# Four batches interleaved in a traced order, with q cast on DVE, full-row tails and k times v per head in column halves

## The chip, the cores and the metric

The kernel runs on one core of one Trainium2 chip. The metric is the device time of one execution in microseconds; lower is better. Engines are named as in the profile: PE is the tensor engine (PEld its weight loads), DVE the vector engine, ACT the scalar engine, POOL the GpSimd engine, SP the engine that issues most transfers. Rounds of different kernels were taken on the same chip in turn.

## The reference

```python
kv  = einsum('bhsd,bhse->bhde', k, v)            # B=8, H=8, S=576, D=64
out = einsum('bhsd,bhde->bhse', q, kv)
x   = out / sqrt(mean(out*out, -1) + 1e-6) * g_norm   # then heads side by side: [B, S, 512]
theta = x @ w_theta
y = w_tok_r @ (x * cos(theta)) + w_tok_i @ (x * sin(theta))   # over tokens
u = x + y
return u + maximum(u @ w_ch, 0)
```

The eight batches are independent. 576 rows are four blocks of 128 and a tail of 64.

## The kernel before

Each batch runs four stages: attention (k·v, transposes of q, q·kv, the norm), phase (transposes of x, theta, sin and cos), mix (token product), channel (last product). The driver interleaves two batches, and the scheduler may reorder within that.

```python
def attention(b):
    kvp = ps([P, HP, P], FP32, f"kv{b}")
    for hp in range(HP):                          # a pair of heads
        pair = slice(2 * hp, 2 * hp + 2)
        ks = work.tile([P, NF, 2, D], FP32, tag="ks", bufs=4, ...)
        nc.gpsimd.tensor_copy(ks[:].rearrange("p j h d -> p h j d"), kt[:, pair, :, :])   # L171
        qs = work.tile([P, NT, 2, D], FP16, tag="qs", bufs=4, ...)
        nc.gpsimd.tensor_copy(qs[:, 0:NF].rearrange(...), qt[:, pair, :, :])
        nc.gpsimd.tensor_copy(qs[:T, NF], ql[:, pair, :])                  # T = 64 rows
        for j in range(NT):
            lhs = ks[:, j, :, :] if j < NF else kl[:, pair, :]
            rhs = vt[:, pair, j, :] if j < NF else vl[:, pair, :]
            nc.tensor.matmul(kvp[:, hp, :], lhs, rhs, ...)                 # L180, half of the result unused
        # transposes of q: four full blocks and two 64x64 ones for the tail (L185)
        ...
    # the two diagonal blocks of kvp go to bd (ACT, L194)
    for ti in range(NT):
        raw = ...                                 # PE, L202: q times bd
        nc.scalar.activation(out=sq, in_=raw, func=AFT.Square)
        nc.vector.reduce_sum(out=ss, in_=sq, ...)
        nc.gpsimd.tensor_scalar(out=ss, in0=ss, scalar1=D * eps, op0=ALU.add)
        nc.gpsimd.tensor_tensor(out=rt, in0=ss, in1=mhalf, op=ALU.pow)
        nc.vector.tensor_tensor(out=xt, in0=raw, in1=rt, op=ALU.mult)      # L219
...
attention(0); load(1, 1); phase(0); token_weights()
for b in range(B):
    if b + 1 < B:
        attention(b + 1)
        if b + 2 < B: load(b + 2, 1)
    if b > 0: channel(b - 1)
    mix(b)
    if b + 1 < B: phase(b + 1)
channel(B - 1)
```

## Time and profile before

381.67 us median of three runs (377.65 to 382.21).

| | busy in one round of 41.64 us | share |
|---|---|---|
| PE | 34.18 us | 82% |
| DVE | 23.97 us | 58% |
| ACT | 19.56 us | 47% |
| POOL | 16.62 us | 40% |

The first fence is from the page of the kernel before: busy microseconds with the share of the span, then 40 equal slices with the busy share in tenths, and the clock granted to PE.

```profile
PE 291.6 (76%) x1965; PEld 176.1 (46%) x1965; DVE 186.2 (49%) x348; ACT 164.4 (43%) x283; POOL 133.5 (35%) x191
...
PE   0097267993996699669968699569968899759895
...
PEclk9999997568798699788997899688997899899999
```

Next, busy time by stretch for one round, taken between equal points of two batches. The columns are the stretch, its length, the busy time of each engine with the number of instructions, the granted clock, the DMA share and GB/s.

```profile
core 0: us, PE busy (x) PEld busy (x) DVE busy (x) ACT busy (x) POOL busy (x), PEclk, DMA share, GB/s
...
187.02:228.66 41.64, 34.18 (x241) 20.39 (x240) 23.97 (x42) 19.56 (x34) 16.62 (x22) 0.88 0.40 115
```

The waits of PE in this round (who waited for whom; us in total, times, longest):

```profile
PE raw_0_1833 L202 <- ACT kvbd_106 L194: 3.8, 1, 3.8
PE vps_4_1982 L330 <- DVE x_3_1887 L219: 1.7, 1, 1.7
PE ups_4_1975 L322 <- DVE x_2_1873 L219: 1.3, 1, 1.3
PE vps_2_1952 L330 <- DVE x_1_1859 L219: 0.7, 1, 0.7
```

And the chain of waits that ended last, by engine:

```profile
PE 43%; DVE 20%; POOL 16%; ACT 10%; DMA 6%; issue 4%; POOLq 0%; DVEq 0%; ACTq 0%
```

No engine is full, and the chain wanders over all of them. PE stands 3.8 us for the eviction of kv and 3.7 us for x in every round. The gaps also cost clock. Right after the 3.8 us wait the q·kv matmuls start 107 ns apart, and at full clock such 128-column matmuls start 56 ns apart. The Trainium skill (TensorE: Matmul & The Clock Gate, Part 1) says that the array falls to half clock after an idle window of about 3.4 us. In this trace less was enough: PE's last matmul before the wait ends at 196.9 us, and the granted clock falls to 0.50 at 199.0 us, 2.1 us later. The mean granted clock of the round is 0.88.

The packed copies and q casts on POOL stretch DVE operations: of these equal instructions (groups by line, shapes kept apart; busy us, mean ns) the first ran beside a q cast on POOL and the second beside nothing.

```profile
L265 DVE TENSOR_SCALAR fa_3_1730<-f_3_1728 128x512 int32<-128x512 int32 x1 | 0.8, 827 | 0.0
...
L265 DVE TENSOR_SCALAR fa_0_1673<-f_0_1671 128x512 int32<-128x512 int32 x1 | 0.4, 421 | 0.0
```

And a k·v group looks like this: eight records of 128 columns for the four blocks of one pair.

```profile
L180 PE MATMUL kv_1754<-v_1459,ks_2_1793 128*128 128x128 f32 x8 | 1.2, 288 | 0.0
```

### The profile page before, as it was taken

To read this page: it belongs to the slowest core of one execution; us is meant where nothing else is said; L and a number is where in the kernel's file an instruction comes from. 1 tells how busy PE (TensorE), PEld (TensorE's weight loads), DVE (VectorE), ACT (ScalarE), POOL (GpSimd) and SP (SyncE) were. 2 spreads that over 40 slices of the span, in tenths; PEclk is the share of its full clock that TensorE was granted. 3 is DMA by queue.
4 is the path that set the end of the run, shared out by engine and by line. 5 is a ranking of instruction groups with operands and counts; after the bars stand their busy time and mean duration, and the time that the engine had idled before them with its cause. 6 is when DMAs were issued, how large, how long until landed. Compare 5 with 4: busy or idle time off the path is not lost.

```text
span 381.3 us, 5161 instructions
## 1 busy us (share of the span) xinstructions
PE 291.6 (76%) x1965; PEld 176.1 (46%) x1965; DVE 186.2 (49%) x348; ACT 164.4 (43%) x283; POOL 133.5 (35%) x191
## 2 busy tenths in 40 slices
PE   0097267993996699669968699569968899759895
PEld 0076125761574256534555357424644357425352
DVE  0001418025494456546484639346564638463954
ACT  1026049340486118711674139610864149513902
POOL 2254640366074503461065406460156300540000
PEclk9999997568798699788997899688997899899999
DMA  8999980069009230753029220502000210021033
GB/s 155 231 323 300 284 236 0 2 160 320 20 8 309 87 95 2 193 167 129 11 87 270 82 58 2 138 27 99 3 0 0 91 35 2 0 80 47 0 125 124
DMA packets 44760, 40.98 MB, mean 107 GB/s; under 512 B 14144, under 2 KB 39360, under 8 KB 44736
## 3 DMA queue, kind: packets, MB, share of 16 engines
q1 hardware_dynamic: 43760, 38.80, 35.8%
q0 software_dynamic: 976, 1.85, 2.7%
q8 instruction: 15, 0.25, 0.3%
q14 instruction: 9, 0.07, 0.1%
HBM read 33.06 MB, written 9.44 MB: 111 GB/s over the span
## 4 chain that ended last, share of the span: by engine, by line
PE 43%; DVE 20%; POOL 16%; ACT 10%; DMA 6%; issue 4%; POOLq 0%; DVEq 0%; ACTq 0%
PE kv_138 L180 3%; PE kv_494 L180 3%; DMA wnat_124<-in_moe_w_tok_i_dram 2%; DMA wnat_123<-in_moe_w_tok_r_dram 2%; PE kv_3089 L180 2%; PE y_0_1102 L303 1%; DMA out_dram<-ot_1_3549 1%; PE y_0_2437 L303 1%; ACT tr_l L284 1%; PE y_0_1547 L303 1%; PE y_0_2882 L303 1%; ACT kvbd_108 L194 1%; ACT kvbd_106 L194 1%; PE y_0_1992 L303 1%; DMA out_dram<-ot_1_3265 1%
## 5 line engine op out<-in xcount | busy, mean ns | idle before, releaser
L180 PE MATMUL kv_138<-v_68,ks_0_139 128*128 128x128 f32 x8 | 2.1, 441 | 19.5 <-POOL ks_0_139 L171 19.5
L109 DVE TENSOR_SCALAR gcol<-gcol 128x1 f32<-128x1 f32 x1 | 0.2, 153 | 25.2 <-DMA gcol<-in_g_norm_dram 25.2
L180 PEld LDWEIGHTS kv_138<-v_68,ks_0_139 128*128 128x128 f32 x8 | 1.8, 328 | 19.5 <-POOL ks_0_139 L171 19.5
L190 ACT COPY qT_0_156<-qTps_0_149 128x640 f16<-128x640 f16 x1 | 0.7, 692 | 21.1 <-PE qTps_0_149 L185 21.1
L214 POOL TENSOR_SCALAR ss_0_3175<-ss_0_3175 128x8 f32<-128x8 f32 x1 | 0.2, 238 | 26.5 <-DVE ss_0_3175 L209 26.5
L242 ACT ACTIVATE xT_741<-xTps_0_742,gcol 128x640 f16<-128x640 f16 x1 | 0.8, 794 | 15.9 <-PE xTps_0_742 L237 15.9
L209 DVE TENSOR_REDUCE ss_0_580<-sq_0_578 128x8 f32<-128x512 f32 x1 | 0.7, 686 | 13.6 <-ACT sq_0_578 L207 13.6
L171 POOL COPY ks_0_1755<-k_1458 128x512 f32<-128x512 f32 x1 | 0.6, 609 | 17.4 <-PE kv_1309 L180 17.4
L171 POOL COPY ks_0_3090<-k_2793 128x512 f32<-128x512 f32 x1 | 0.6, 609 | 17.4 <-PE kv_2644 L180 17.4
L171 POOL COPY ks_0_2200<-k_1903 128x512 f32<-128x512 f32 x1 | 0.6, 609 | 16.3 <-PE kv_1754 L180 16.3
L171 POOL COPY ks_0_2645<-k_2348 128x512 f32<-128x512 f32 x1 | 0.6, 609 | 16.1 <-PE kv_2199 L180 16.1
L242 ACT ACTIVATE xT_299<-xTps_0_300,gcol 128x640 f16<-128x640 f16 x1 | 0.8, 794 | 11.9 <-PE xTps_0_300 L237 11.9
L171 POOL COPY ks_0_865<-k_643 128x512 f32<-128x512 f32 x1 | 0.6, 610 | 14.9 <-PE kv_494 L180 14.9
L306 PE MATMUL yl_656<-wT_428,z_0_345 128*128 128x64 f16 x4 | 0.9, 230 | 6.4 <-DVE uT_655 L310 6.4
L303 PEld LDWEIGHTS <-z_l 128*128 128x128 f16 x32 | 3.3, 103 | 3.9 <-issue 0.8
L171 POOL COPY ks_0_1310<-k_1013 128x512 f32<-128x512 f32 x1 | 0.9, 904 | 11.8 <-PE kv_864 L180 11.8
L209 DVE TENSOR_REDUCE ss_0_224<-sq_0_222 128x8 f32<-128x512 f32 x1 | 0.7, 686 | 8.6 <-ACT sq_0_222 L207 8.6
L327 ACT COPY u_0_3688<-ups_0_3683 128x512 f16<-128x512 f16 x1 | 0.6, 586 | 9.7 <-PE ups_0_3683 L322 9.7
L330 PEld LDWEIGHTS <-uT_655 128*128 128x128 f16 (+1 forms) x20 | 2.2, 119 | 5.4 <-issue 3.8
L242 ACT ACTIVATE xT_1186<-xTps_0_1187,gcol 128x640 f16<-128x640 f16 x1 | 0.8, 793 | 8.6 <-PE xTps_0_1187 L237 8.6
L250 PEld LDWEIGHTS <-xT_299 128*128 128x128 f16 x20 | 2.4, 126 | 4.5 <-issue 2.9
L242 ACT ACTIVATE xT_2521<-xTps_0_2522,gcol 128x640 f16<-128x640 f16 x1 | 0.8, 793 | 8.6 <-PE xTps_0_2522 L237 8.6
(1960 smaller groups left out, 1187.3 us busy)
## 6 DMA issues: line engine op xcount, KB each, us to landing
k_67<-in_k_dram SPq DMA_DIRECT2D x4, 256.0 KB, 9.3
v_68<-in_v_dram SPq DMA_DIRECT2D x4, 256.0 KB, 10.5
q_69<-in_q_dram SPq DMA_DIRECT2D x4, 256.0 KB, 10.1
k_287<-in_k_dram SPq DMA_DIRECT2D x1, 1024.0 KB, 7.1
v_288<-in_v_dram SPq DMA_DIRECT2D x1, 1024.0 KB, 8.3
q_289<-in_q_dram SPq DMA_DIRECT2D x1, 1024.0 KB, 11.2
k_643<-in_k_dram SPq DMA_DIRECT2D x1, 1024.0 KB, 10.2
v_644<-in_v_dram SPq DMA_DIRECT2D x1, 1024.0 KB, 9.9
```

The source lines that it names most:

```text
L171: nc.gpsimd.tensor_copy(ks[:].rearrange("p j h d -> p h j d"), kt[:, pair, :, :])
L180: nc.tensor.matmul(kvp[:, hp, :], lhs, rhs, start=(j == 0), stop=(j == NT - 1))
L190: nc.scalar.copy(out=t[:], in_=pq[:])
L194: nc.scalar.copy(out=bd[r * D:(r + 1) * D, :, r * D:(r + 1) * D], in_=kvp[r * D:(r + 1) * D, :, r * D:(r + 1) * D],)
L209: nc.vector.reduce_sum(out=ss[:], in_=sq[:].rearrange("p (h e) -> p h e", h=H), axis=mybir.AxisListType.X,)
L242: nc.scalar.activation(out=xT[:, kc, :], in_=px[:], func=AFT.Copy, scale=gcol[:])
L250: nc.tensor.matmul(th[:], xT[:, kc, ti * P:(ti + 1) * P], wth[:, kc, :], start=(kc == 0), stop=(kc == NK - 1),)
L284: nc.scalar.activation(out=tr[:], in_=f[:], func=AFT.Sin, scale=-RAD, bias=tail_bias[:])
L303: nc.tensor.matmul(y[:], lhs, wT[n][:, 0:SF], start=(n == 0), stop=(n == 2 * NF))
L306: nc.tensor.matmul(yl[:, kc, :], lhs, wT[n][:, SF:S], start=(n == 0), stop=(n == 2 * NF))
L327: nc.scalar.copy(out=u[:rows], in_=pu[:rows])
L330: nc.tensor.matmul(vp[:rows], uT[:, kc, ti * P:ti * P + rows], wch[:, kc, :], start=(kc == 0), stop=(kc == NK - 1),)
```

## The change

The intent: let stages of four batches interleave in one order that is traced by a virtual clock (each stage of batch b has a window in rounds of 28 us), and hold every engine to that order; and take work off PE and POOL. k·v is now computed per head, each head's 64 columns in one half of the array, which needs no packed copy of k and computes no unused half; q is cast on DVE; tails are padded to full rows so that no 64-row matmul is left in k·v and in the transposes. The core of the diff, with cuts:

```diff
+ROUND = 28.0
+WINDOWS = {"cast": (-1.0, 13.0), "attention": (0.0, 14.0), "norm": (17.0, 44.0), "turn": (45.0, 53.0),
+    "phase": (52.0, 78.0), "mix": (82.0, 110.0), "channel": (112.0, 140.0)}
+def in_traced_order(tc):                 # each instruction after the last one traced on its engine
+    ...
-    psA = ctx.enter_context(tc.tile_pool(name="psA", bufs=8, ...))
+    PS = {"kv": 1, "raw": 2, "tp": 2, "mm": 3}          # PSUM banks
-            nc.gpsimd.tensor_copy(ks[:].rearrange("p j h d -> p h j d"), kt[:, pair, :, :])
-            nc.gpsimd.tensor_copy(qs[:, 0:NF]..., qt[:, pair, :, :])
+        nc.vector.tensor_copy(st["qs", b][:, 0:NF, 2 * hp:2 * hp + 2, :]..., qs[hp][:])
-                nc.tensor.matmul(kvp[:, hp, :], lhs, rhs, ...)
+            for r in range(2):
+                nc.tensor.matmul(
+                    kvp[r * D:(r + 1) * D, hp, :],
+                    ks[hp][:, r, j, :] if j < NF else kl[:, 2 * hp + r, :],
+                    vs[hp][:, r, j, :] if j < NF else vl[:, 2 * hp + r, :],
+                    start=(j == 0), stop=(j == NT - 1),
+                )
-            for (j, rows, at) in blocks:                # 4 full blocks, 2 of 64 rows
+        for j in range(NT):                             # 5 full blocks
                 nc.tensor.matmul(pq[...], ..., is_transpose=True, ...)
...
+    load(0)
+    load_theta()
+    for b in range(B):
+        if b > 0:
+            put((b - 0.9) * ROUND, once(load, b))
+        for (name, (stage, n)) in stages.items():
+            (lo, hi) = WINDOWS.get((name, b), WINDOWS[name])
+            for i in range(n):
+                put(b * ROUND + lo + (hi - lo) * i / n, stage(b, i))
+    put(0.9 * ROUND, once(load_mixers))
+    ...                                                 # stages run in order of virtual time
+    in_traced_order(tc)
```

Also the token mix is split in halves of 288 columns in place of 512 and 64, q, k and v are loaded per pair of heads (a q tail twice), the token weights are loaded later, and the eight PSUM banks are given to fixed uses (1, 2, 2 and 3).

## The prediction

> **What bounds it now.** No engine: the order does. The chain of waits repeats: 41.9, 41.6, 42.9 and 42.4 us between equal points of batches 3 to 7. From 187.0 to 228.7 us (busy time by stretch) PE is busy 34.2 us, DVE 24.0, ACT 19.6, POOL 16.6. The chain that ended last is PE 43%, DVE 20%, POOL 16%, ACT 10%: one batch's norm (square, reduce, pow of 1.67 us, scale) and phase run while PE has little other work. The PE timeline shows 3.8 us waiting for the kv eviction and 3.7 us for x per batch, and gaps cost clock: mean granted 0.88, raw matmuls 107 ns apart instead of 56. The first k·v matmul starts at 19.5 us, behind 16.8 us of token-weight loads on the chain.
>
> **What changes.** Four batches interleave, so PE finds work during those waits. Per batch, from full-clock spacings in the PE timeline:
> - k·v: 40 records 150 ns apart, tails slower (0.21 us): 6.3 us now. Afterwards 80 records with half the columns. The Trainium skill (TensorEngine Tiling (Array Packing), Key Properties) says different tiles run in parallel but a mode switch drains the array; no run shows it yet. Estimate 4.5 us (3 if the halves overlap, 6.5 if not).
> - q and x transposes: 2 x 1.96 us to 2 x 1.1, as half-row tails go.
> - token mix: 36 x 0.216 + 36 x 0.028 = 8.8 us to 72 x 0.122 = 8.8 us (estimate).
> - raw 1.1, theta 4.3, channel 5.4: unchanged.
>
> PE sum about 27 us (29.5 now, without waits and cold clock).
> - DVE: the q cast comes, 5 x 128x512 f32, estimated at the 0.42 us of the 128x512 bit-and: 2.1 us. POOL's copies (7.4 us) go, and with them the DVE operations stretched beside them (0.74 to 1.06 us instead of 0.42). DVE about 25 us; POOL keeps 9.5, ACT 20.
> - Token weights load later; a q tail is loaded twice.
>
> **On the critical path.** Nearly all of it: the round becomes the larger of PE 27 and DVE 25 us, plus stalls of in-order queues: 29.5 us instead of 42. By the traced windows a batch spans five rounds: four filling, four full, four draining. Filling is bound by loads: 3.7 MB per batch plus weights at the 250 to 300 GB/s of the first 60 us gives 75 to 85 us until the fifth batch starts. Full: 4 x 29.5 = 118 us. Draining: PE sums of 20, 18, 13 and 5 us plus latency, about 70 us. End transfer 4 us.
>
> **Predicted: 275 us, range 255 to 305 (8 in 10). Faster by over 2%: 0.97; within: 0.02; slower: 0.01.**
>
> **What would show each step.** PE busy over 85% with a granted clock above 0.95 in the middle; rounds of 28 to 31 us; first k·v matmul before 10 us; k·v group 3 to 6.5 us per batch; cast at 0.42 us (0.7 at half rate, DVE then 26.5); no bit-and above 0.5 us; PE's waits for x and kvbd gone.
>
> **What would make it wrong.** A fixed order stalls one engine on another (PE on a bank that ACT or DVE still reads: two transposing, three product banks), rounds then being 33 us or more; column halves that do not overlap and drain the array at each switch; loads and stores sharing one queue, a waiting load delaying stores; filling slower than loads allow, from latency and a cold clock.

## More of the kernel before

The kernel before shows runs near 376 us and near 382 us, the latter with a lower mean granted clock (0.89 and 0.93 are typical), and the later ones of that kind were counted as slow.

The profiled run spans 381.3 us: it took 383.09 us at a mean granted clock of 0.886, so it is like the runs that were later counted as slow. The rounds and waits of the kernel before are read from it and may be up to some 2% too long (the fast runs are near 376 to 378 us).

## The result

286.76 us median of four runs (286.23 to 288.16); before, 379.66 us (376.42 to 382.21). The ratio is 0.758, with a 95% interval from 0.750 to 0.766. Ratios here are the mean time of one kernel's fast runs over that of the other's of the same rounds, so not quite the ratio of the medians. The profiled run spans 284.7 us.

The lines of the page after that answer to those before (busy, slices, clock, chain by engine):

```profile
PE 226.5 (80%) x2221; PEld 154.7 (54%) x2221; DVE 191.8 (67%) x396; ACT 168.6 (59%) x283; POOL 81.0 (28%) x91
...
PE   1053463866489888998999899989999988999994
...
PEclk9997575599859999999999999999999999999999
...
PE 36%; DVE 25%; ACT 16%; POOL 10%; issue 5%; DMA 5%; SPq 2%; ACTq 0%; DVEq 0%
```

Busy time by stretch, cut at the kv eviction of each batch (found to 0.5 us; the DMA share adds up the time that packets took, and can pass 1), so that each line but the last is one round; two middle rounds, equal to the one shown, are left out:

```profile
core 0: us, PE busy (x) PEld busy (x) DVE busy (x) ACT busy (x) POOL busy (x), PEclk, DMA share, GB/s
0.00:24.50 24.50, 7.05 (x100) 5.85 (x101) 4.51 (x17) 5.97 (x9) 0.69 (x6) 1.00 0.90 234
24.50:45.00 20.50, 9.96 (x124) 8.11 (x123) 7.02 (x14) 5.85 (x12) 10.97 (x13) 0.60 1.06 251
45.00:72.00 27.00, 17.54 (x198) 12.39 (x199) 15.85 (x36) 18.28 (x31) 9.80 (x10) 0.80 1.09 278
72.00:98.00 26.00, 20.01 (x199) 13.38 (x198) 18.38 (x39) 17.50 (x30) 9.64 (x10) 0.80 0.46 115
98.00:123.50 25.50, 23.26 (x255) 16.11 (x253) 21.68 (x46) 18.88 (x33) 9.61 (x10) 1.00 0.38 98
123.50:151.00 27.50, 26.06 (x274) 17.80 (x273) 23.01 (x49) 20.03 (x35) 9.60 (x10) 1.00 0.63 173
...
206.00:284.70 78.70, 70.53 (x534) 45.50 (x532) 55.29 (x107) 41.98 (x71) 11.46 (x12) 1.00 0.20 69
```

The longest wait of PE in the middle, from 123 to 206 us, which are three rounds and have three such waits:

```profile
PE ups_4_2139 L366 <- ACT xT_2078 L296: 0.8, 1, 0.8
...
```

And the groups that changed: the sixteen k·v records of one pair (two heads), one bit-and, one cast.

```profile
L230 PE MATMUL kv_1768<-v_2_1376,k_2_1375 128*64 128x64 f32 x16 | 0.7, 228 | 0.0
...
L325 DVE TENSOR_SCALAR fa_2_1957<-f_2_1955 128x512 int32<-128x512 int32 x1 | 0.4, 426 | 0.0
...
L216 DVE CAST qs_1745<-q_1_1371 128x512 f16<-128x512 f32 x1 | 0.4, 418 | 0.0
```

The middle is a different machine: rounds of 27.5 us with PE busy 26.07 (95%), clock 1.00, no waits for x or kv left, and 1.4 us of idle PE a round. The first five rounds are not: PE is busy 7.05 + 9.96 + 17.54 + 20.01 + 23.26 = 77.8 of their 123.5 us. Of the 58 us in which PE idles in the whole span, 45.7 lie there, 4.3 in the middle and 8.2 at the end.

### The profile page after: what moved, and what is told of

Its sections match the earlier page's. It is cut to its first block, busy times and chain, and to the rows that moved or that the text cites. A ratio compares the mean times of both kernels' runs of the same rounds, so it can differ in the third digit from the quotient of the medians.

```text
span 284.7 us, 5734 instructions
## 1 busy us (share of the span) xinstructions
PE 226.5 (80%) x2221; PEld 154.7 (54%) x2221; DVE 191.8 (67%) x396; ACT 168.6 (59%) x283; POOL 81.0 (28%) x91
## 4 chain that ended last, share of the span: by engine, by line
PE 36%; DVE 25%; ACT 16%; POOL 10%; issue 5%; DMA 5%; SPq 2%; ACTq 0%; DVEq 0%
DMA k_2_118<-in_k_dram 2%; DMA wst_133<-in_moe_w_theta_dram 2%; SPq L135 1%; DMA wst_142<-in_moe_w_theta_dram 1%; SPq L143 1%; ACT xT_3328 L296 1%; ACT xT_2541 L296 1%; ACT xT_2078 L296 1%; ACT xT_2975 L296 1%; ACT xT_1615 L296 1%; PE y_0_878 L351 1%; ACT xT_806 L296 1%; ACT xT_1172 L296 1%; DVE uT_3415 L356 1%; ACT wth L170 1%
## 5 line engine op out<-in xcount | busy, mean ns | idle before, releaser
L170 ACT ACTIVATE wth<-wst_133 128x512 f16<-128x512 f32 x1 | 0.6, 630 | 15.0 <-DMA wst_133<-in_moe_w_theta_dram 15.0
L238 PE MATMUL qTps_0_159<-ident_75,qs_145 128*128 128x128 f16 x5 | 0.7, 309 | 9.0 <-DVE qs_145 L216 9.0
L238 PEld LDWEIGHTS <-qs_145 128*128 128x128 f16 x20 | 1.5, 116 | 10.4 <-DVE qs_145 L216 9.2
L267 DVE TENSOR_REDUCE ss_0_262<-sq_0_260 128x8 f32<-128x512 f32 x1 | 0.7, 686 | 8.1 <-ACT sq_0_260 L264 8.1
L238 PEld LDWEIGHTS <-qs_288 128*128 128x128 f16 x20 | 1.6, 125 | 6.1 <-DVE qs_288 L216 6.0
L230 PE MATMUL kv_148<-v_0_103,k_0_102 128*64 128x64 f32 x16 | 1.1, 319 | 4.4 <-DMA v_0_103<-in_v_dram 4.4
L304 PEld LDWEIGHTS <-xT_1172 128*128 128x128 f16 x20 | 1.9, 98 | 4.0 <-ACT xT_1172 L296 2.3
L304 PEld LDWEIGHTS <-xT_806 128*128 128x128 f16 x20 | 1.9, 106 | 3.4 <-ACT xT_806 L296 2.4
L230 PE MATMUL kv_148<-vl_68,kl_67 128*64 128x64 f32 x16 | 1.6, 296 | 2.7 <-DMA vl_68<-in_v_dram 2.7
L238 PEld LDWEIGHTS <-qs_528 128*128 128x128 f16 x20 | 1.1, 98 | 4.4 <-DVE qs_528 L216 4.2
L304 PEld LDWEIGHTS <-xT_2975 128*128 128x128 f16 x20 | 1.9, 98 | 2.7 <-ACT xT_2975 L296 0.7
L304 PEld LDWEIGHTS <-xT_3328 128*128 128x128 f16 x20 | 1.9, 98 | 2.7 <-ACT xT_3328 L296 0.7
L230 PEld LDWEIGHTS kv_148<-v_0_103,k_0_102 128*64 128x64 f32 x16 | 1.0, 221 | 4.4 <-DMA k_0_102<-in_k_dram 4.4
L258 PE MATMUL raw_2_291<-kvbd_89,qT_0_165 128*128 128x128 f16 x1 | 0.3, 288 | 3.8 <-DVE x_0_267 L278 3.8
L291 PE MATMUL xTps_0_441<-ident_75,x_4_438 128*128 128x128 f16 x1 | 0.3, 287 | 3.8 <-DVE x_4_438 L278 3.8
L304 PEld LDWEIGHTS <-xT_2078 128*128 128x128 f16 x20 | 1.9, 98 | 2.5 <-ACT xT_2078 L296 0.7
L304 PEld LDWEIGHTS <-xT_2541 128*128 128x128 f16 x20 | 1.9, 98 | 2.5 <-ACT xT_2541 L296 0.7
L304 PEld LDWEIGHTS <-xT_1615 128*128 128x128 f16 x20 | 1.9, 98 | 2.5 <-ACT xT_1615 L296 0.7
L304 PEld LDWEIGHTS <-xT_440 128*128 128x128 f16 x20 | 1.9, 105 | 2.3 <-ACT xT_440 L296 0.7
L304 PE MATMUL th_0_870<-wth,xT_806 128*128 128x512 f16 x4 | 2.3, 619 | 1.0 <-ACT xT_806 L296 1.0
## 6 DMA issues: line engine op xcount, KB each, us to landing
wnat_97<-in_moe_w_tok_i_dram POOLq DMA_DIRECT2D x1, 576.0 KB, 11.7
```

What stands on the lines that cost most here:

```text
L170: nc.scalar.activation(out=wth[:, kc, :], in_=wst[:], func=AFT.Copy, scale=FOLD)
L230: nc.tensor.matmul(kvp[r * D:(r + 1) * D, hp, :], ks[hp][:, r, j, :] if j < NF else kl[:, 2 * hp + r, :], vs[hp][:, r, j, :] if j < NF els ...
L238: nc.tensor.matmul(pq[:, j * P:(j + 1) * P], st["qs", b][:, j, pair, :], ident16[:], is_transpose=True, start=(j == 0), stop=(j == NT - 1),)
L258: nc.tensor.matmul(raw[:, hp * P:(hp + 1) * P], st["qT", b, hp][:, ti * P:(ti + 1) * P], bd[:, hp, :], start=(hp == 0), stop=(hp == HP - 1),)
L267: nc.vector.reduce_sum(out=ss[:], in_=sq[:].rearrange("p (h e) -> p h e", h=H), axis=mybir.AxisListType.X,)
L291: nc.tensor.matmul(px[:, ti * P:(ti + 1) * P], st["x", b, ti][:, kc * P:(kc + 1) * P], ident16[:], is_transpose=True, start=(ti == 0), sto ...
```

## The experiments

Two theories were to be told apart in two places. In the middle: (A) PE sets the round, so PE work counts one for one; rivals: the waits of the fixed order, or DVE, set it. In the filling: (O) the fixed order, with its chain through POOL and DVE, sets the first rounds; rival: the loads do, as the prediction said. Rounds below are distances of kv evictions in the traces; "middle" means the last three of them.

| Run | Median us | Ratio to before | Middle round, us |
|---|---|---|---|
| changed kernel | 286.76 | 0.758 | 27.5 |
| parts_only | 356.75 | 0.942 | 39.7 |
| weave_only | 335.93 (fast runs 332.65, 333.55) | 0.881 | 32.3 |
| kv_by_head | 291.19 | 0.770 | 28.5 |
| kv_pairs | 311.18 | 0.823 | 30.8 |
| qcast_pool | 292.46 | 0.775 | 28.5 |
| half_tails | 296.74 | 0.785 | 28.8 |
| free_order | 302.09 | 0.796 | 31.7 |
| cheap_pow (wrong result) | 278.27 (fast runs 276.37, 274.83) | 0.729 | 27.3 |
| theta_split | 282.46 | 0.749 | 27.5 |
| fill_v1 | 303.31 | 0.805 | 27.0 |
| no_v_loads (wrong result) | 279.78 | 0.740 | 27.5 |
| x_later | fast runs 280.15, 278.41 | none given | 27.3 |

The profiled runs of weave_only and cheap_pow fell in the slow state (under 2% longer than their fast runs), so only their middle rounds, at a clock of 1.00, are read closely; what is said below of the filling of cheap_pow comes from that slow run and is weaker. One of the four runs of free_order was slow too (305.63 us). The record gives no clear verdict ("unclear") for theta_split, fill_v1 and no_v_loads, though the intervals of their ratios to the kernel before lie far below one (0.746 to 0.752, 0.802 to 0.809 and 0.733 to 0.747). The runs were taken in several sets on different chips, so small differences between rows of different sets are less sure than those within one.

### The order and the parts, each alone

parts_only is the kernel before with the three parts and its own order and scheduler:

```diff
-                nc.tensor.matmul(kvp[:, hp, :], lhs, rhs, start=(j == 0), stop=(j == NT - 1))
+                for r in range(2):
+                    h = 2 * hp + r
+                    nc.tensor.matmul(kvp[r * D:(r + 1) * D, hp, :], kt[:, h, j, :] ..., vt[:, h, j, :] ..., ...)
-            nc.gpsimd.tensor_copy(ks..., kt...)          # no packed copy
-            nc.gpsimd.tensor_copy(qs..., qt...)
+            nc.vector.tensor_copy(qs..., qt...)
-            for (j, rows, at) in blocks: ...             # full-row tails for q, x and k, v
+            for j in range(NT): ...
```

> The kernel before with the parts of the change and without its order: k times v per head in the two column halves (no packed copy of k on POOL), q cast on DVE, full-row tails; stages in the old sequence, the scheduler orders. Theory W (the old rounds are set by waits of one batch's chain, so less work on PE gains only where PE's work is on that chain): PE work falls by about 5 us per batch, and k times v and the transposes are on the chain, so about 3 to 5 us per round are gained: 345 to 360 us. Rival P (the parts carry most of the gain): under 325 us. Rival N (the saved work only lengthens waits): over 372 us.

weave_only is the changed kernel with the parts of before (its windows and traced order, k·v as pairs with the packed copy, q cast on POOL, 64-row tails). It keeps the finer loads, the later token weights, the bank split and the halves of the token mix, so "order alone" below includes these; its first k·v starts at 11.7 us, against 19.5 us before.

```diff
-                nc.tensor.matmul(kvp[r * D:(r + 1) * D, hp, :], ks[hp][:, r, j, :] ..., ...)
+            nc.tensor.matmul(kvp[:, hp, :], kp[:, j, :, :] if j < NF else kl[0:T, pair, :], ...)
+        nc.gpsimd.tensor_copy(kp[:].rearrange("p j h d -> p h j d"), ks[hp][:])
-        nc.vector.tensor_copy(st["qs", b]..., qs[hp][:])
+        nc.gpsimd.tensor_copy(st["qs", b]..., qs[hp][:])
-        for j in range(NT): ...                          # and the same for x
+        for (j, rows, at) in blocks: ...
```

> The changed kernel's order with the parts of before: k times v as pairs with the packed copy on POOL, q cast on POOL, 64-row tails. Theory W (the woven order carries most of the gain, and once PE is full the parts' PE work adds one for one): PE about 26 + 3.1 + 2.3 = 31.5 us per batch, rounds about 32.5 us, total 318 to 330 us. Rival P (the parts carry it, order alone gains little): over 350 us. Rival I (independent gains): whatever is added by half_tails, kv_pairs and qcast_pool to 287 us is the sum here.

One middle round of each by stretch, parts_only first:

```profile
214.00:253.50 39.50, 29.62 (x272) 17.05 (x272) 23.09 (x51) 19.30 (x35) 9.52 (x10) 0.90 0.24 72
```

```profile
192.00:224.50 32.50, 30.37 (x242) 20.71 (x241) 22.40 (x43) 20.40 (x36) 15.17 (x19) 1.00 0.56 152
```

The waits of PE over three middle rounds of parts_only:

```profile
PE raw L210 <- ACT kvbd L202: 13.7, 3, 4.6
PE vps L337 <- DVE x L227: 10.7, 9, 2.1
```

Theory W held for the parts alone (356.75 us lies in its 345 to 360), and for the order it was a little optimistic (333 against 318 to 330). The old order has the same two waits as before, kv eviction and x: 24.4 us in three rounds, 8.1 a round against 7.5 before. PE busy falls from 34.2 to 30.1 us (the mean of the three rounds), and the round by only 2 us, from 41.6 to 39.7: the other half of the saved PE work becomes idle time of PE. In the woven order, PE busy falls from 30.2 to 26.1 us when the parts come in and the round falls from 32.3 to 27.5. (More than the 4.1 us of PE work, because a wait of PE for the packed copy on POOL, 3.8 us in the three rounds of weave_only, goes too.) The order alone shortens the round by 9.3 us. Of these, 4.0 are busy time of PE on nearly the same matmuls (34.2 to 30.2 us, 241 and 242 records), as the granted clock rises from 0.88 to 1.00, and 5.3 are idle time. Rival I, that the costs of the parts add up, comes near: the three undone parts below add 5.6 us to the round of the changed kernel, which gives 33.1 us against 32.3, and 40 us to its total, 327 against 333. Order and parts together do more than the product of each alone: parts alone 0.942, order alone 0.881, product 0.830, both together 0.758.

### Undoing one part at a time

kv_pairs: k·v in pairs again. The packed copy on POOL came back with it. kv_by_head keeps the per-head form but does not alternate the halves:

```diff
-        for j in range(NT):
-            for r in range(2):
+        for r in range(2):
+            for j in range(NT):
                 nc.tensor.matmul(kvp[r * D:(r + 1) * D, hp, :], ...)
```

> The changed kernel with the k times v matmuls of a pair of heads in another order: all five blocks of one head (one column half of the array), then all five of the other, instead of alternating the halves block by block. Same matmuls, same data. Theory A (alternating halves run side by side in the array; the 33 ns spacing of the 80 records is two overlapped 66 ns ones): spacing within a head becomes about 65 ns, the group of a pair goes from 0.73 to about 1.35 us, 2.5 us more PE work per batch, rounds in the middle 27.4 to about 29.5 us, total about 287 + 16 = 303 us. Rival B (a record with 64 columns simply costs a quarter of one with 128, 33 ns whatever the order): nothing changes, 287 us. Rival C (halves overlap, but PE is not what sets the round, the woven order's waits are): group grows as in A, total within 3 us of 287.

The k·v records alone in three middle rounds, the changed kernel first and then kv_by_head (240 records each):

```profile
123.50:206.00 82.50, 9.62 (x240) 7.96 (x240) 1.00 0.54 154
```

```profile
125.00:210.50 85.50, 14.39 (x240) 12.74 (x240) 1.00 0.50 145
```

The halves do run side by side. The same 240 records take 14.39 us when one half follows itself and 9.62 when the halves alternate. The starts in the packed traces show how. In kv_by_head the records of one half start 58 ns apart. In the changed kernel they start in pairs, 6 to 7 ns apart, with 58 ns from one pair to the next (and a first gap of 107 ns in either run): 29 ns a record, against 111 ns for a 128-column record at full clock in kv_pairs below. Over a whole group of 20 the means are 31 and 51 ns; 51 and not 58, because in kv_by_head the first records of the second head start between the last ones of the first. (The trace does not name the half of a record; that a pair is one record of each half is read from the order in the kernel.) Theory A was right in kind, and the effect smaller than it said (it expected 65 ns, 1.35 us a group and 303 us): 1.6 us more k·v time a round, PE busy up 1.3 us (82.17 in place of 78.20 in three rounds), the round up 1.0 us, the total up 4.4. Rival B (order of the records does not matter) falls; so does rival C. This agrees with the Trainium skill (TensorEngine Tiling (Array Packing), Key Properties), which says that different tiles run in parallel; what the run adds to it is that here neighbouring instructions had to be in different tiles.

> The changed kernel with k times v of two heads in one 128x128 product again, as before, with the packed copy of k on POOL that it needs; order, q cast on DVE and full-row tails stay. Theory A (PE is 95 percent busy in the middle rounds, so its work is the round): k times v goes from 2.9 back to about 6 us per batch at full clock, the round from 27.4 to about 30 us, and the copies on POOL (4 x 0.61 us) stretch some DVE operations; total 305 to 312 us. Rival C (waits of the order set the round): under 292 us.

```diff
-                nc.tensor.matmul(kvp[r * D:(r + 1) * D, hp, :], ks[hp][:, r, j, :] ..., vs[hp][:, r, j, :] ..., ...)
+            nc.tensor.matmul(kvp[:, hp, :], kp[:, j, :, :] ..., vs[hp][:, :, j, :] ..., ...)
+        kp = work.tile([P, NF, 2, D], FP32, tag="kp", bufs=4, ...)
+        nc.gpsimd.tensor_copy(kp[:].rearrange("p j h d -> p h j d"), ks[hp][:])
```

PE's largest wait in three middle rounds of kv_pairs:

```profile
PE kv L233 <- POOL kp L221: 5.5, 3, 1.8
```

Here PE busy rises by 1.8 us a round (83.63 - 78.20, over three), and PE waits another 1.8 us for the packed copy, which stands on POOL behind the pow. Together this is about the 3.3 us that the round grows, to 30.8. (One of the three rounds had a granted clock of 0.95 and took 31.5 us; the other two took 30.5 us with PE busy 27.5.) The total, 311.18 us, is in theory A's range, but half of the effect is the copy that the per-head form makes unnecessary.

> The changed kernel with the five q casts of a batch back on POOL (before they took 0.76 us each there), everything else kept. DVE loses 5 x 0.42 = 2.1 us per batch. Theory A (PE sets the middle rounds, DVE at 84 percent is second): middle rounds within 0.5 us of 27.4, total 283 to 292 us; the pow on POOL now waits behind casts and some DVE operations stretch, so filling may be a little slower. Rival D (DVE's in-order queue sets the round): rounds drop to about 26.5 us, total under 281 us. Rival E (moving the cast was needed: POOL's pow delayed[...]): rounds above 29 us, total over 298 us.

```diff
-            nc.vector.tensor_copy(st["qs", b][:, NF], ql[:])
+            nc.gpsimd.tensor_copy(st["qs", b][:, NF], ql[:])
-        nc.vector.tensor_copy(st["qs", b][:, 0:NF, ...], qs[hp][:])
+        nc.gpsimd.tensor_copy(st["qs", b][:, 0:NF, ...], qs[hp][:])
```

PE's largest wait in three middle rounds, and the bit-ands of one round on DVE:

```profile
PE qTps L238 <- POOL qs L216: 4.2, 3, 1.4
```

```profile
L325 DVE TENSOR_SCALAR fa<-f 128x512 int32<-128x512 int32 x4 | 2.6, 640 | 0.1
```

The result, 292.46 us, lies at the upper edge of A's total range and outside its round (28.5 us against 27.4 plus or minus 0.5); rivals D and E both fall. PE's own work did not change (77.96 in place of 78.20 us in three rounds), so this 1 us is a new wait: 4.2 us in three rounds for the q cast on POOL. DVE gave away 15 casts, 6.3 us in three rounds, and its busy time fell by 0.9 us, because others stretched: the mean bit-and is 640 ns in place of 426. This mean mixes two kinds. Of the twelve of 128x512 in three middle rounds, six take 426 or 427 ns and six 846 to 855. All of the long ones ran beside a cast on POOL; of the short ones, three ran beside none and three beside a cast that itself took 852 to 857 ns in place of some 610. So of two that met, either the bit-and was doubled or the cast was lengthened by 40%, not both. The Trainium skill (GPSIMD Engine Reference, Specifications) says that GpSimd shares its SBUF interfaces with the vector engine, with contention for DVE instructions in a two-port mode or with two SBUF inputs. These lengths agree with such a sharing; no run here shows in which mode the bit-and, which has one input, runs.

> The changed kernel with the 64-row tails of before in k times v and in the q and x transposes (two 64x64 transposes in place of one full, the tail product over 64 rows). Theory A: about 0.2 us more per transpose group of 8 groups, and a slower tail of each of the 4 k times v groups, some 2.3 us of PE per batch; middle rounds about 29.5 us, total 300 to 306 us. Rival: the array takes 64-row work beside 128-row work without cost and total stays within 3 us of 287.

```diff
-        for j in range(NT):
-            nc.tensor.matmul(pq[:, j * P:(j + 1) * P], st["qs", b][:, j, pair, :], ident16[:], ...)
+        for (j, rows, at) in blocks:
+            nc.tensor.matmul(pq[:, at:at + rows], st["qs", b][:rows, j, pair, :], ident16[:rows, :rows], ...)
```

(the same for x, and kl[0:T], vl[0:T] in k·v.) PE busy rises by 1.9 us a round (83.94 - 78.20, over three) and the round by 1.3 us, to 28.8; 296.74 us in total, below A's 300 to 306 and far from the rival's "within 3 us". PE is then busy 97% of the round: there is little left but PE work.

In all of these but qcast_pool, PE work put back comes back as time: 1.0 us of round for 1.3 us of work in kv_by_head, 1.3 for 1.9 in half_tails, and in kv_pairs, without its new wait, 1.5 for 1.8. That is what a nearly full PE looks like: about three quarters come back, the rest fills small waits.

### Is the fixed order needed?

> The changed kernel without the dependencies that hold each engine to the traced order: the scheduler may reorder as it does in the kernel before. Theory T (the fixed order matters): the scheduler's order is worse than the traced one, rounds 29 to 32 us, total 295 to 320 us. Rival S (the woven trace is enough, the scheduler keeps close to it): within 6 us of 287 us. Rival F (the fixed order is what makes filling slow, as a first q cast waits behind a scale of the norm weights): filling until the fifth batch's first k times v falls from 112 us to under 95 us, total under 275 us.

```diff
-    in_traced_order(tc)
```

PE's largest wait in its three middle rounds:

```profile
PE y L351 <- DVE ot L381: 5.5, 5, 2.3
```

Theory T held: 302.09 us, middle rounds of 31.7 us, PE busy 83.19 of 95.0 us. The woven trace alone is not enough; left free, the scheduler moves work so that PE waits for product banks that DVE has yet to read. Rival F falls: the fifth kv eviction came within 0.5 us of 123.5 us with the fixed order and without. So holding the engines to the order is not what makes the filling slow; the scheduler, left free, fills no faster.

### What makes the filling slow

The chain of one norm tile can be read from the timeline of the changed kernel. Columns: start, length, engine, line, operation; in brackets the idle time before it and what ended that.

```profile
37.76 0.60 ACT L264 ACTIVATE sq_3_377<-raw_3_370 128x512 f32<-128x512 f32 x1
...
38.38 0.69 DVE L278 TENSOR_TENSOR x_2_368<-raw_2_291,rt_2_318 128x512 f16<-128x512 f32 x1 [3.00 <-POOL rt_2_318 L275]
...
39.32 0.68 DVE L267 TENSOR_REDUCE ss_3_380<-sq_3_377 128x8 f32<-128x512 f32 x1
...
40.41 1.67 POOL L275 TENSOR_TENSOR rt_3_383<-ss_3_380,mhalf 128x8 f32<-128x8 f32 x1
42.11 0.69 DVE L278 TENSOR_TENSOR x_3_403<-raw_3_370,rt_3_383 128x512 f16<-128x512 f32 x1 [2.11 <-POOL rt_3_383 L275]
42.71 0.42 DVE L216 CAST qs_288<-q_3_193 128x512 f16<-128x512 f32 x1
...
43.19 0.71 PE L238 MATMUL qTps_3_416<-ident_75,qs_288 128*128 128x128 f16 x5 [2.54 <-DVE qs_288 L216]
...
44.37 0.60 ACT L264 ACTIVATE sq_4_427<-raw_4_422 128x512 f32<-128x512 f32 x1 [3.73 <-PE raw_4_422 L258]
```

The reduce of tile 3 stands behind the scale of tile 2, which waits for POOL; the q cast stands behind the scale of tile 3; PE's transpose needs that cast, and the next raw product stands behind the transpose. So from the square of tile 3 at 37.76 us to that of tile 4 at 44.37 us pass 6.6 us, in which PE is busy 3.4 us, in part at half clock (a mean of 0.76; the last matmuls start some 107 ns apart), and waits 3.2 us for the two q casts.

> The changed kernel with the pow on POOL (1.67 us each) replaced by a multiply of the same tiles (about 0.25 us); wrong result on purpose. It shortens the chain square, reduce, pow, scale of each norm tile by 1.4 us. Theory Q (the filling rounds, 30.9, 25.4, 28.7 and 27.4 us long with PE busy only 8.7 to 24.2 us, are bound by five norm tiles one after the other in the fixed order): the third and fourth round lose about 5 us each, the middle rounds, where PE is 95 percent busy, under 1 us: total 272 to 279 us. Rival L (loads bind filling): under 3 us gained. Rival M (the pow chain also binds middle rounds): they fall to 26 us, total under 270 us.

```diff
-        nc.gpsimd.tensor_tensor(out=rt[:], in0=ss[:], in1=mhalf[:], op=ALU.pow)
+        nc.gpsimd.tensor_tensor(out=rt[:], in0=ss[:], in1=mhalf[:], op=ALU.mult)
```

The fast runs, 276.4 and 274.8 us, are in theory Q's range. The evictions of batches 0 to 4 come at 23, 43, 69, 93 and 118.5 us, against 24.5, 45, 72, 98 and 123.5: 5 us are gained in the filling, and the middle rounds are 27.3 us against 27.5. The third and fourth round lose 1 and 2 us, not the 5 each that Q expected, so in this run pow is one link of the chain, not the chain. But the profiled run was a slow one. The fast runs are 4 to 5 us shorter, and no trace shows in which round; how much pow costs the filling stays open. (Q cut its rounds at the first k·v of each batch. By that cut the first four rounds of the changed kernel end at 30.9, 56.3, 85.0 and 110.6 us, so its fourth is 25.5 us, not 27.4; in cheap_pow they end at 28.1, 52.3, 82.0 and 105.7.)

theta_split moves the scale of the norm weights on DVE and those of the theta weights on ACT later in the traced order, because in the changed kernel the first q cast stands behind them. The waits, from the changed kernel:

```profile
DVE gcol L164 <- DMA gcol<-in_g_norm_dram: 13.0, 1, 13.0
...
PE qTps_0_159 L238 <- DVE qs_145 L216: 9.0, 1, 9.0
...
PE raw_2_291 L258 <- DVE x_0_267 L278: 3.8, 1, 3.8
PE xTps_0_441 L291 <- DVE x_4_438 L278: 3.8, 1, 3.8
```

The last two are the longest waits of PE between the first and the fifth eviction (24.5 to 123.5 us). In all that time no wait of PE's matmuls ends with a load, and its weight loads wait 0.8 us in all for one.

> The changed kernel with one thing moved: the scale of the norm weights (DVE) and the four scales of the theta weights (ACT) come later in the traced order (at 16 us of it, before the first norm tile), their loads stay where they are, with four buffers in place of two. In the trace of the changed kernel the first q cast starts at 16.9 us, behind the scale of the norm weights that waits 13.0 us for its load, and the third theta load is issued at 17.7 us behind ACT. Theory O (the fixed order makes the start slow): first kv eviction falls from 24.5 to 18 to 20 us, the second from 45 to about 41, total 3 to 6 us less, 281 to 284 us. Rival L (loads bind the first two rounds whatever the order): first eviction earlier, but the second within 1 us of 45 us and total within 1.5 us of 287 us.

```diff
-    load_theta()            # loads, gcol scale on DVE, four scales on ACT, 2 buffers
+    load_theta()            # loads only, 4 buffers
+    put(16.0, once(scale_theta))
```

282.46 us (281.47 to 282.72; no overlap with the changed kernel's runs, ratio 0.749 against 0.758). The first eviction comes at 17 us and the fifth at 119.5, as theory O said, the first even a little earlier. But this run also lets SP issue the next loads sooner, so it does not exclude loads as the limit. no_v_loads does that; it is theta_split with v not loaded at all:

> As theta_split, with v not loaded: the product is k times k; wrong result on purpose. A third fewer bytes are loaded per batch (2.4 MB less the tails in place of 3.7 MB), all engines do the same work in the same order. In theta_split the kv evictions of batches 0 to 4 come at 17, 39.5, 68.5, 94 and 119.5 us, with the DMA engines near full until 68 us. Theory L (loads bind filling): first eviction at about 13, second at about 29, third below 56 us, total about 270 us. Theory O (the fixed order with its chain through POOL binds): first eviction 2 to 3 us earlier, third no more than 5 us earlier, rounds three to five unchanged (25 to 29 us), total 276 to 280 us.

```diff
-            for (dst, src) in ((kt, k), (vt, v), (qt, q)):
+            for (dst, src) in ((kt, k), (qt, q)):
-            vs.append(vt)
+            vs.append(kt)
```

The second to fourth stretch of the filling of theta_split, then of no_v_loads (DMA share and GB/s last):

```profile
17.00:39.50 22.50, 9.56 (x124) 7.80 (x123) 7.23 (x14) 8.47 (x16) 10.97 (x13) 0.64 1.05 266
39.50:68.50 29.00, 20.00 (x196) 13.70 (x197) 15.41 (x35) 17.88 (x31) 9.78 (x10) 0.68 1.13 276
68.50:94.00 25.50, 20.61 (x201) 12.90 (x200) 18.47 (x39) 17.52 (x31) 9.89 (x10) 0.82 0.37 105
```

```profile
14.00:36.50 22.50, 9.54 (x124) 7.80 (x123) 7.24 (x14) 8.47 (x16) 10.97 (x13) 0.63 1.14 253
36.50:66.00 29.50, 21.21 (x198) 14.14 (x199) 15.32 (x36) 18.09 (x31) 9.78 (x10) 0.65 0.59 152
66.00:92.00 26.00, 20.01 (x198) 13.28 (x197) 18.23 (x39) 17.35 (x30) 9.63 (x10) 0.80 0.23 68
```

With about a third fewer bytes (24.7 MB read in place of 34.1) only the first round is shorter, by 3 us (14 in place of 17). The others are 22.5, 29.5, 26 and 25.5 us against 22.5, 29, 25.5 and 25.5, although the DMA share of the third falls from 1.13 to 0.59. In the second it stays high (1.14), so for that round the equal length says less, but there too PE's waits end with x, q casts and the kv eviction, not with loads. Theory L falls: a DMA system that looked full did not set the pace after the first round. The total, 279.78 us, is in theory O's range.

Two attempts to change the order so that it fills faster:

> As theta_split, and the windows of batches 0, 1 and 2 moved: their norm, turn, phase, mix and channel come earlier in the traced order, so that batch 0 is through its phase and mix while the loads of batches 1 and 2 arrive; batches 3 to 7 keep their windows. Same work. Theory O (filling is slow because the order holds back work that could run while loads arrive: PE is busy 43 of the first 85 us): PE's idle time of the first 110 us shrinks by 10 to 18 us and, as the middle rounds are PE-bound, the total falls by as much against theta_split: 266 to 274 us. Rival L (loads bind until 71 us and engines after it): under 4 us gained against theta_split. Rival Z (bank or buffer waits between the shifted batches): slower than theta_split.

```diff
+    ("norm", 0): (14.0, 27.0), ("turn", 0): (29.0, 32.0), ("phase", 0): (33.0, 50.0), ("mix", 0): (66.0, 92.0), ...
+    ("norm", 1): (15.0, 34.0), ("turn", 1): (35.0, 39.0), ("phase", 1): (40.0, 62.0), ("mix", 1): (68.0, 94.0), ...
+    ("norm", 2): (16.0, 38.0), ("turn", 2): (39.0, 45.0), ("phase", 2): (46.0, 70.0), ("mix", 2): (75.0, 102.0), ...
```

PE's waits between 23 and 125 us:

```profile
PE raw L279 <- DVE x L299: 13.7, 6, 4.1
PE qTps L259 <- DVE qs L237: 6.7, 5, 2.1
PE xTps L312 <- DVE x L299: 5.2, 3, 3.1
```

This failed: 303.31 us, 21 us slower than theta_split. The second and third rounds became 32.5 and 34.5 us, as PE waited 13.7 us for raw banks that x had not yet left, and 11.9 us for casts and x. Rival Z held. Bringing one batch's chain forward put the next batch's attention behind it. So the order of the trace can make the filling slower, and an earlier window is not a better order.

> As theta_split, with the scale of each norm tile (x on DVE) traced 1.8 us later, so that DVE does other work while POOL's pow runs, rather than stand at x; same work. In the trace of the changed kernel DVE waits 2.1 to 3.0 us at each x of the first batches, and PE's transposes wait for q casts that stand behind it. Theory O1 (the place of x in DVE's order lengthens the filling chain): filling 3 to 6 us shorter than theta_split, middle rounds unchanged at 27.5, total 276 to 280 us. Rival O2 (the chain goes through x itself, as the next raw product needs x's bank: only two raw banks): no change or up to 5 us longer, 281 to 288 us.

```diff
-        yield 2.8
+        yield 4.6          # x is traced 1.8 us later
```

The fifth eviction comes at 117 us in place of 119.5, less than theory O1 expected. Two runs were fast (280.15 and 278.41 us) and two slow (282.96, 283.25): inconclusive in the total, small in any case. theta_split beats the kernel before clearly and the changed one by 1.5%; its runs do not overlap with those of the changed kernel, but they come from another set on another chip, and the difference is under 2%.

## Why the prediction was right

The time lies in the range, 286.8 against 275 (255 to 305), and the mechanism of the middle rounds was right. That of the filling was not, and two other errors made up for most of it, which is luck. Point by point:

- **"No engine: the order does"**: right. With the old parts and the new order alone the round falls from 41.6 to 32.3 us.
- **The round becomes the larger of PE 27 and DVE 25 us plus stalls, 29.5 us**: right in kind, too long. PE is 26.1, DVE 23.0 us, the round 27.5 us. The stalls are 1.4 us, not 2.5. The undone parts show that PE is nearly the bound.
- **k·v at 3 to 6.5 us, estimated 4.5**: it takes 3.2 us a batch (9.62 over three). The halves overlap (29 ns a record when they alternate, 58 ns in one half). The 150 ns that it took for a 128-column record had part of the slow tails in it; kv_pairs shows 111. The drain at mode switches that it feared is small: a k·v group starts 216 ns after the last record of a token product, and in kv_pairs, where nothing switches, 123 ns after it; at the end of a group it is much the same. So a switch costs some 0.1 us and the eight of a batch 0.8 us (an estimate from these starts).
- **Cast at 0.42 us, no bit-and above 0.5 us in the middle, DVE about 25**: cast 0.42, bit-and 0.43, DVE 23.0 us.
- **Transposes 1.1 us, token mix even at 0.122 us a matmul, PE over 85% busy, clock above 0.95, first k·v before 10 us**: as predicted (95%, 1.00, 4.4 us). PE's waits for x and kv are gone in the middle but not in the filling.
- **Filling bound by loads, 75 to 85 us until the fifth batch starts**: this step failed. The first k·v of the fifth batch starts at 110.5 us, 30 us late. Removing a third of the loads shortens only the first round, by 3 us, and after it PE waits for x and q casts, not for loads. So the pace is set by chains of waits between engines. Three links were tried: pow (5 us, in a slow run), the early scales (4 us) and the place of x (2.5 us on top). They were not tried together, and some 18 of the 30 us are not accounted for by any run. Not holding the order does not shorten it either (free_order). The prediction listed this among its risks ("filling slower than loads allow, from latency and a cold clock") but priced it at nothing.
- **Four full rounds 118 us, draining 70 and end transfer 4**: measured 110 (4 x 27.5) and 284.7 - 110.5 - 110 = 64 us. These two terms were 8 and 10 us too large and by luck hid most of the filling's 30 us. The total was therefore closer than its parts.

What stays open: which part of the 38 us of PE idle time that theta_split still has in its first 119.5 us is a necessary latency and which an order could hide. fill_v1 shows that moving whole windows, in the one way tried, does not do it. Open too is the part of the cold clock: the second to fourth stretch of the changed kernel had mean granted clocks of 0.60, 0.80 and 0.80, and no run changes that alone. In free_order the third and fourth stretch ran at 1.00 and took 22 and 20 us, but the fifth took 29.5 and the fifth eviction came no sooner.

## What to carry to other kernels

When stages of one work item alternate between engines, weave several items first: here about half of the work taken off an engine that waits only became idle time, while after the weave 4.1 us less of PE work, with the wait for a copy that went with it, shortened the round by 4.8 us in place of 2. Judge a woven, fixed order in two parts, middle and filling, because in the filling an instruction that waits in a fixed order holds up unrelated ones behind it, as the q casts here stood behind x, and a busy DMA row there proves nothing until loads are taken away or the waits are read. Alternate the column halves instruction by instruction, not head by head (9.62 us against 14.39 for the same records).

## What the Trainium skill lacked or had wrong

- TensorEngine Tiling (Array Packing), Key Properties and Theoretical Speedup: it says that tiles run in parallel, with up to 2x, but not that neighbouring instructions must alternate between tiles, and has no float32 figure. Here float32 records of a 64-column half start 58 ns apart in one half and come to 29 ns each when the halves alternate (two start 6 to 7 ns apart, every 58 ns), and 111 ns apart as 128-column ones.
- The same page, Key Properties: a mode switch drains the array, without a price. Here about 0.1 us a switch (an estimate from start times: 216 ns from a token product to k·v with a switch, 123 ns without).
- GPSIMD Engine Reference: no price for a pow. Here 1.67 us for 128x8 elements of float32, in every norm tile's chain; an add of the same tile is 0.24 us.
- GPSIMD Engine Reference, Specifications: this section names the contention without a size. Here a 128x512 bit-and on DVE took 426 ns, or some 850 ns beside a cast on POOL, or else the cast took some 855 ns in place of 610.
